# An attention and two-layer expert kernel: the low halves of the expert weights are formed on one engine instead of two

## The chip, the cores and the metric

The kernel runs on one core of one Trainium2 chip. The metric is the device time of one execution in microseconds. Three executions of the kernel before took 867.55, 1329.99 and 867.36 us, so the median is 867.55 us; the profiled execution took 865.88 us.

## The reference

Three stages follow each other on 3072 tokens (4 batches of 768) of 512 numbers.

```python
# 1. attention in chunks of 32 positions over 56 neighbours and 8 memory keys, 8 heads of 64
scores = scale * np.matmul(q_c, k_full.transpose(0, 1, 3, 2))
out[:, :, c_start:c_end] = np.matmul(softmax(scores), v_full)
# 2. a dense layer, 512 -> 2048 -> 512
h = x @ w_in
x = (h * np.cos(h)) @ w_out
# 3. eight experts, 512 -> 1024 -> 512, one per token, skipped where x @ w_skip <= 0
e_idx = np.argmax(xc @ w_gate, axis=1)
h = np.maximum(xc[mask] @ w1[e], 0.0)
y[mask] = gate_w[mask, None] * (h @ w2[e])
out[do_compute] = xc + y
```

## The kernel before

All products of the dense layer and of the experts are formed in three passes: each operand is split into a high part (rounded to fp32r) and a low part (what the rounding left), and high x high, high x low and low x high are added in PSUM. A weight piece is 128 x 1024 numbers (512 KB). For the experts, `plan_piece32` (L920) plans one piece `m`: SyncE loads it into a `raw` buffer (four of them, L930), ScalarE copies each half `s` of 512 columns to the high part (`copy`, L239), and a subtraction raw - high gives the low part (L939). Eight pieces make an expert; a piece with an even number holds a quarter of w1, one with an odd number a quarter of w2.

An expert's work on TensorE: L381 transposes its 128-token tiles of rows, L581 forms h for 128 hidden units of two tiles (12 matmuls of 256 columns; L1045 and L1055 do it for experts with one tile), ScalarE makes the high part `gh` (L1014), VectorE the low part `gl` (L1017), and L999 multiplies both by w2 (two groups of three matmuls of 512 columns, `gh` twice and `gl` last). L1087 on VectorE then joins the result with the tokens, and L1091 on GpSimd scatters it to `out`; each scatter waits for the one before it to have landed. L385 on VectorE makes the low part of the next expert's rows.

The order of every engine's queue is fixed ahead of time: each operation is a `Task` with an engine, an assumed duration and a key, and `Schedule.run` (L121) plays them through, always taking the ready task with the smallest key. The played order is written down, and the chip's engines then run their queues strictly in it. A changed engine or assumed duration of a task can therefore move other tasks too.

Before, the subtraction of half 1, and of both halves of the first `M_EARLY` = 18 pieces, is on VectorE; half 0 of the other 46 pieces is on GpSimd, in the same queue as the scatters L1091. Experts run in the order of their places 0 to 7; places 3 and 7 have one tile of tokens, place 0 treats its two tiles one after the other, the others take two tiles together. Place 2 is the first of which a half is subtracted on GpSimd.

Of the kernel before, what the change touches and what calls it, by code (L numbers as in the profile page):

```python
# [9 lines left out]
F32 = mybir.dt.float32  # L10
# [6 lines left out]
ALU = mybir.AluOpType  # L17
# [31 lines left out]
LEAD = 2.5  # L49
WARM = 12  # L50
EARLY = 16
M_EARLY = 18
RAW = 4
HOLD = (14, 16)
PACE = 8
# [42 lines left out]
class Schedule:  # L98
# [7 lines left out]
    def add(self, eng, dur, key, fn, after=(), new=(), use=(), table=None, nbytes=None):  # L106
        t = Task(eng, dur, key, fn, new, use, table, nbytes)
        for s in t.slots:
            s.users += 1
        for p in after:  # L110
            p.kids.append(t)
            t.wait += 1
        self.tasks.append(t)
        return t
# [75 lines left out]
def kernel(  # L190
# [13 lines left out]
    nc = tc.nc  # L204
# [33 lines left out]
    def copy(out, in_, scale=1.0):  # L238
        nc.scalar.activation(out=out, in_=in_, func=AF.Copy, scale=scale)  # L239
# [22 lines left out]
    def slot(name):  # L262
        return Slot(groups.setdefault(name, Group(1)))
# [5 lines left out]
    dve = lambda *a, **k: add("DVE", *a, **k)  # L269
    gps = lambda *a, **k: add("Pool", *a, **k)  # L270
# [20 lines left out]
    def warm_exp():  # L291
# [10 lines left out]
        out=first_slot, in0=eoff, scalar1=ident[:, 0:1], scalar2=None, op0=ALU.mult), [t_cb])  # L302
# [41 lines left out]
    for z in range(2):  # L344
        for i, name in enumerate(("k", "v")):
# [3 lines left out]
            use = [big[i]] if z else []  # L349
# [486 lines left out]
    w2_slot, w2_ready, w2_used, outs, regs = {}, {}, {}, [], {}  # L836
# [83 lines left out]
    def plan_piece32(m, key):  # L920

        o = {}
        s_raw, s_w = slot("raw"), slot("w")
        w2_slot[m] = s_w
        src = m % 2 * (NF2 // 2) + m % NF2 // 2

        def ld():
            o["r"] = pools["mp"][1].tile([P, 1024], F32, tag="raw", name="raw", bufs=RAW)
            piece = w12[bass.ds(regs[m // NF2] * NF2 + src, 1)]
            nc.sync.dma_start(out=o["r"], in_=piece.rearrange("o p c -> p (o c)"))  # L930

        def alloc():
            wt["x", m] = wp.tile([P, 2, 1024], F32R, tag="w", name="w", bufs=16)

        half = lambda s: o["r"][:, 512 * s:512 * s + 512]
        part = lambda s, i: wt["x", m][:, i, 512 * s:512 * s + 512]

        def lo(eng, s):
            eng.tensor_tensor(out=part(s, 1), in0=half(s), in1=part(s, 0).bitcast(F32), op=ALU.subtract)  # L939

        early = m < M_EARLY
        hold = [] if m < M_HOLD else [last["placed"]]
        w = mark(key, alloc, [last["mp"]] + hold, new=[s_w])
        after = [last["mp"], last["reg", m // NF2]] + ([w2_used[m - PACE]] if m >= PACE else [])
        x = load(key - 2, ld, P * 4096, after, new=[s_raw])
        w2_ready[m] = []
        for s in range(2):
            eng, put, dur = (nc.vector, dve, 0.6) if s or early else (nc.gpsimd, gps, 1.23)
            h = act(0.52, key + s * 0.5, lambda s=s: copy(part(s, 0), half(s)), [x, w], use=[s_raw, s_w])
            w2_ready[m].append(put(dur, key + s * 0.5, lambda s=s, eng=eng: lo(eng, s), [h], use=[s_raw, s_w]))  # L950

    def plan_rows(p, t, key, after):

# [179 lines left out]
    for c in range(NCH):  # L1133
        key = at[c // 2, NF - 1] + 1.7
# [35 lines left out]
    for p, t, j, key in todo:  # L1170
        mine = NF2 * p + 2 * (j if t is not None else j // 2) + 1
        while planned <= mine:
            plan_piece32(planned, keys[planned] - 5)
            planned += 1
        if t is None:
            plan_unit2(p, j, key)
        else:
            plan_pair(p, t, j, key)
# [156 lines left out]
```

## Time and profile before

| what | value |
|---|---|
| three executions | 867.55, 1329.99, 867.36 us |
| the profiled execution, whole | 865.88 us |
| its span, first to last instruction | 864.1 us |
| TensorE busy | 823.9 us, 95% |
| VectorE, ScalarE, GpSimd busy | 595.9, 525.5, 312.5 us |
| mean granted TensorE clock | 0.980 |
| DMA in all | 106.09 MB, mean 123 GB/s |

The attention and the dense layer take the span up to about 665 us; the experts run from there to 852 us. PE is TensorE, DVE VectorE, ACT ScalarE, POOL GpSimd and SP SyncE; a releaser behind an arrow is what ended the engine's idle time. Start times are microseconds from the span's start. A TensorE row's duration is modelled and overlaps the next row, so the distance between the starts of rows is what counts there.

### The profile page before, as it was taken

Reading aid. Unit: us, or ns where it says so; the run is one execution under the profiler, and the core shown is the slowest. Engines: PE = TensorE matmul, PEld = TensorE weight load, DVE = VectorE, ACT = ScalarE, POOL = GpSimd, SP = SyncE. Lnnn points to the kernel's source line nnn. Section 1 sums busy time; section 2 is a strip of 40 time slices with the busy share of each in tenths; the row PEclk is TensorE's granted clock in tenths of the full one; section 3 lists DMA queues with packets and bytes.
Section 4 is the critical chain, followed back from the end, with each engine's and each line's share of the span. In section 5 each row is a group of like instructions: output and inputs, shape, how many; then the busy total and the mean of one; then the engine's idle time right before and its main releaser. Section 6 shows DMA issues by size and latency. Waiting matters only on the chain.

```text
span 864.1 us, 17777 instructions
## 1 busy us (share of the span) xinstructions
PE 823.9 (95%) x6408; PEld 718.1 (83%) x6408; DVE 595.9 (69%) x1552; ACT 525.5 (61%) x1204; POOL 312.5 (36%) x376
## 2 busy tenths in 40 slices
PE   7799899999999999999999999999999899999884
PEld 4688788878888888888888888888888799989773
DVE  7778885799749376583956749376596476896761
ACT  6778876555757566565655757566666465665341
POOL 5456454333323223232232232223233114675441
PEclk9799999999999999999999999999999999999998
DMA  9449545722223131321322214121312466685530
GB/s 344 160 141 281 152 138 198 217 76 76 67 66 96 32 99 35 85 70 33 104 60 62 70 49 111 35 62 28 122 57 90 176 237 233 214 303 208 175 121 29
DMA packets 37201, 106.09 MB, mean 123 GB/s; under 512 B 6747, under 2 KB 7003, under 8 KB 36976
## 3 DMA queue, kind: packets, MB, share of 16 engines
q1 hardware_dynamic: 34064, 98.74, 37.1%
q0 software_dynamic: 3040, 6.13, 2.0%
q8 instruction: 52, 0.85, 0.4%
q14 instruction: 45, 0.37, 0.1%
HBM read 88.10 MB, written 20.77 MB: 126 GB/s over the span
## 4 chain that ended last, share of the span: by engine, by line
PE 79%; DVE 7%; ACT 4%; DMA 4%; issue 3%; POOL 1%; SPq 1%; DVEq 0%; POOLq 0%; ACTq 0%
PE pb L581 35%; PE py L585 26%; PE py L999 7%; PE pb L449 4%; PE pb L1045 2%; DVE junk L688 2%; PE pb L381 1%; DMA flat<-in_kt_dram 1%; DVE w L939 1%; ACT w L239 1%; PE pb L473 1%; DVE u L620 1%; DMA xg<-xs 1%; DMA more<-in_qt_dram 1%; DVE ki L609 1%
## 5 line engine op out<-in xcount | busy, mean ns | idle before, releaser
L581 PE MATMUL pb<-xh,w 128*128 128x256 f32 x1856 | 268.8, 288 | 7.5 <-ACT xh L239 3.9
L628 POOL TENSOR_TENSOR gl<-u,gh 128x256 fp32r<-128x256 f32 x192 | 146.8, 765 | 351.1 <-ACT gh L239 266.6
L581 PEld LDWEIGHTS pb<-xh,w 128*128 128x128 f32 x1856 | 249.6, 192 | 28.7 <-DVE u L620 6.5
L585 PE MATMUL py<-w,gh 128*128 128x512 f32 x768 | 244.9, 400 | 0.6 <-ACT yt L239 0.3
L688 DVE SCALAR_TENSOR_TENSOR junk<-yt,wg 128x512 bf16<-128x512 f32 x198 | 149.3, 754 | 7.4 <-ACT yt L239 4.9
L585 PE MATMUL py<-w,gl 128*128 128x512 f32 x384 | 150.8, 393 | 0.7 <-POOL gl L628 0.7
L581 PE MATMUL pb<-xl,w 128*128 128x256 f32 x928 | 149.7, 284 | 0.0
L585 PEld LDWEIGHTS py<-w,gh 128*128 128x128 f32 x768 | 132.4, 190 | 20.6 <-ACT gh L239 1.7
L609 DVE SCALAR_TENSOR_TENSOR ki<-pb,ki 128x256 f32<-128x256 f32 x192 | 80.5, 419 | 84.6 <-ACT ki L239 84.2
L620 DVE SCALAR_TENSOR_TENSOR u<-ki,pb 128x256 f32<-128x256 f32 x192 | 79.9, 417 | 75.0 <-ACT ki L616 72.7
L581 PEld LDWEIGHTS pb<-xl,w 128*128 128x128 f32 x928 | 128.6, 193 | 0.0
L239 ACT ACTIVATE ki<-pb 128x256 int32<-128x256 f32 x192 | 72.8, 380 | 88.1 <-PE pb L581 68.8
L613 ACT ACTIVATE ki<-ki 128x256 f32<-128x256 f32 x192 | 79.7, 416 | 62.2 <-DVE ki L609 62.0
L239 ACT ACTIVATE gh<-u 128x256 fp32r<-128x256 f32 x192 | 79.4, 414 | 58.4 <-DVE u L620 51.8
L939 DVE TENSOR_TENSOR w<-raw,w 128x512 fp32r<-128x512 f32 x82 | 85.8, 1060 | 21.0 <-ACT w L239 20.5
L585 PEld LDWEIGHTS py<-w,gl 128*128 128x128 f32 x384 | 72.3, 188 | 20.0 <-POOL gl L628 3.4
L239 ACT ACTIVATE w<-raw 128x512 fp32r<-128x512 f32 x128 | 74.9, 625 | 14.4 <-DMA raw<-in_w_dram 13.6
L616 ACT ACTIVATE ki<-ki 128x256 f32<-128x256 f32 x192 | 79.6, 415 | 4.6
L939 POOL TENSOR_TENSOR w<-raw,w 128x512 fp32r<-128x512 f32 x46 | 60.5, 1326 | 45.9 <-ACT w L239 45.4
L999 PE MATMUL py<-w,gh 128*128 128x512 f32 x224 | 72.8, 406 | 0.0
L560 POOL TENSOR_TENSOR w<-cv,w 128x512 fp32r<-128x512 f32 x32 | 41.2, 1290 | 38.3 <-ACT w L239 36.8
L999 PE MATMUL py<-w,gl 128*128 128x512 f32 x112 | 45.5, 406 | 5.3 <-DVE gl L1017 5.1
(152 smaller groups left out, 859.4 us busy)
## 6 DMA issues: line engine op xcount, KB each, us to landing
raw<-in_w_dram SPq DMA_DIRECT2D x64, 512.0 KB
k<-in_kt_dram SPq DMA_DIRECT2D x40, 256.0 KB
v<-in_vw_dram SPq DMA_DIRECT2D x40, 256.0 KB
st<-in_w_in_dram SPq DMA_DIRECT2D x16, 512.0 KB
st<-in_w_out_dram SPq DMA_DIRECT2D x16, 512.0 KB
out_dram<-yt SPq DMA_DIRECT2D x96, 64.0 KB
q<-in_qt_dram SPq DMA_DIRECT2D x21, 256.0 KB
xs<-fl SPq DMA_DIRECT2D x8, 528.0 KB
```

What stands on the lines that cost most here:

```text
L239: nc.scalar.activation(out=out, in_=in_, func=AF.Copy, scale=scale)
L560: nc.gpsimd.tensor_tensor(out=wt[f][:, i, 1, :], in0=o["f"], in1=wt[f][:, i, 0, :].bitcast(F32), op=ALU.subtract)
L581: nc.tensor.matmul(ph, w[:, i, ct, :], x[j][:, ct, :], start=(n == 0), stop=(n == len(todo) - 1))
L585: nc.tensor.matmul(py, g[i][:, t * P:t * P + P], w[:, j, :], start=(first and n == 0), stop=(last and n == 2))
L609: nc.vector.scalar_tensor_tensor(out=o["v"], in0=o["p"], scalar=INV2PI / W_SCALE, in1=o["k"], op0=ALU.mult, op1=ALU.subtract)
L613: nc.scalar.activation(out=o["v"], in_=o["v"], func=AF.Sin, scale=math.pi)
L616: nc.scalar.activation(out=o["v"], in_=o["v"], func=AF.Square, scale=math.sqrt(2.0))
L620: nc.vector.scalar_tensor_tensor(out=o["u"], in0=o["v"], scalar=1.0, in1=o["p"], op0=ALU.subtract, op1=ALU.mult)
L628: nc.gpsimd.tensor_tensor(out=o["g"][1], in0=o["u"], in1=o["g"][0].bitcast(F32), op=ALU.subtract)
L688: nc.vector.scalar_tensor_tensor(out=junk, in0=o["y"][:, 0:DM], scalar=1.0, in1=state["wg"][:, j, :], op0=ALU.mult, op1=ALU.mult, accum_ou ...
L939: eng.tensor_tensor(out=part(s, 1), in0=half(s), in1=part(s, 0).bitcast(F32), op=ALU.subtract)
L999: nc.tensor.matmul(ey[p, t], g[i][:, cols], w[:, j, 512 * (f % 2):512 * (f % 2) + 512], start=(f == 0 and q == 0), stop=(f == n - 1 and q ...
```

## The change

`M_EARLY` goes, and the subtraction L939 has one engine: all 128 of them (64 pieces, two halves) are on VectorE, none on GpSimd. The assumed duration that the planner uses for them becomes 0.62 us (it was 0.6 on VectorE, 1.23 on GpSimd).

```diff
-M_EARLY = 18
@@
-        def lo(eng, s):
-            eng.tensor_tensor(out=part(s, 1), in0=half(s), in1=part(s, 0).bitcast(F32), op=ALU.subtract)
-
-        early = m < M_EARLY
+        def lo(s):
+            nc.vector.tensor_tensor(out=part(s, 1), in0=half(s), in1=part(s, 0).bitcast(F32), op=ALU.subtract)
+
@@
         for s in range(2):
-            eng, put, dur = (nc.vector, dve, 0.6) if s or early else (nc.gpsimd, gps, 1.23)
             h = act(0.52, key + s * 0.5, lambda s=s: copy(part(s, 0), half(s)), [x, w], use=[s_raw, s_w])
-            w2_ready[m].append(put(dur, key + s * 0.5, lambda s=s, eng=eng: lo(eng, s), [h], use=[s_raw, s_w]))
+            w2_ready[m].append(dve(0.62, key + s * 0.5, lambda s=s: lo(s), [h], use=[s_raw, s_w]))
```

In the changed kernel's rows line numbers are 1 less (up to this function) or 3 less (behind it): the subtraction is L938, `gl` L1014, L385 is L384, L581 is L580, L999 is L996, and the scatter is L1088.

VectorE's queue while the expert of place 5 runs, before (`w<-raw,w` is the subtraction, `gl` the low part of an activation, `xl` that of the rows of place 6):

```order
L939 TENSOR_TENSOR w<-raw,w 128x512
L1017 SCALAR_TENSOR_TENSOR gl<-pb,gh 128x256
L939 TENSOR_TENSOR w<-raw,w 128x512
L1017 SCALAR_TENSOR_TENSOR gl<-pb,gh 128x256
L385 TENSOR_TENSOR xl<-pb,xh 128x4x128
L939 TENSOR_TENSOR w<-raw,w 128x512
L385 TENSOR_TENSOR xl<-pb,xh 128x4x128
L939 TENSOR_TENSOR w<-raw,w 128x512
L1017 SCALAR_TENSOR_TENSOR gl<-pb,gh 128x256 x2
```

The same place now:

```order
L938 TENSOR_TENSOR w<-raw,w 128x512 x2
L1014 SCALAR_TENSOR_TENSOR gl<-pb,gh 128x256
L938 TENSOR_TENSOR w<-raw,w 128x512 x2
L1014 SCALAR_TENSOR_TENSOR gl<-pb,gh 128x256
L938 TENSOR_TENSOR w<-raw,w 128x512
L384 TENSOR_TENSOR xl<-pb,xh 128x4x128
L938 TENSOR_TENSOR w<-raw,w 128x512
L384 TENSOR_TENSOR xl<-pb,xh 128x4x128
L938 TENSOR_TENSOR w<-raw,w 128x512 x2
L1014 SCALAR_TENSOR_TENSOR gl<-pb,gh 128x256 x2
```

Ahead of each `gl` there now stand two subtractions, both halves of a piece, where one stood.

GpSimd's queue over the experts of places 4 to 7, before (subtractions, and the scatters of finished rows):

```order
L1091 DMA out_dram<-ot,ri 3072x512
L939 TENSOR_TENSOR w<-raw,w 128x512 x8
L1091 DMA out_dram<-ot,ri 3072x512
L939 TENSOR_TENSOR w<-raw,w 128x512
L1091 DMA out_dram<-ot,ri 3072x512
L939 TENSOR_TENSOR w<-raw,w 128x512 x7
L1091 DMA out_dram<-ot,ri 3072x512
L939 TENSOR_TENSOR w<-raw,w 128x512
L1091 DMA out_dram<-ot,ri 3072x512
L939 TENSOR_TENSOR w<-raw,w 128x512 x7
L1091 DMA out_dram<-ot,ri 3072x512 x3
```

GpSimd's queue now, from the last rows of the dense layer to the end of the experts:

```order
L675 MEMSET yt 128x7
L676 COPY yt<-cb 128x1
L675 MEMSET yt 128x7
L676 COPY yt<-cb 128x1
L743 DMA xs<-yt,si 24704x528 x2
L1088 DMA out_dram<-ot,ri 3072x512 x14
```

GpSimd has only the fourteen scatters left; nothing stands behind one that waits.

TensorE's queue changes at one place, where the one-tile expert of place 3 hands over to place 4. Before (`cb,xg` is the transpose of place 4's second tile of rows):

```order
L381 MATMUL pb<-cb,xg 128x128 x4
L999 MATMUL py<-w,gh 128x512 x2
L999 MATMUL py<-w,gl 128x512
L1055 MATMUL pb<-cb,u 128x128 x2
L999 MATMUL py<-w,gh 128x512 x2
L999 MATMUL py<-w,gl 128x512
L581 MATMUL pb<-xh,w 128x256 x8
L581 MATMUL pb<-xl,w 128x256 x4
```

Now:

```order
L1052 MATMUL pb<-cb,u 128x128 x2
L996 MATMUL py<-w,gh 128x512 x2
L996 MATMUL py<-w,gl 128x512
L996 MATMUL py<-w,gh 128x512 x2
L996 MATMUL py<-w,gl 128x512
L380 MATMUL pb<-cb,xg 128x128 x4
L996 MATMUL py<-w,gh 128x512 x2
L996 MATMUL py<-w,gl 128x512
L996 MATMUL py<-w,gh 128x512 x2
L996 MATMUL py<-w,gl 128x512
L580 MATMUL pb<-xh,w 128x256 x8
L580 MATMUL pb<-xl,w 128x256 x4
```

The transpose and place 4's first h moved behind more of place 3's products; the count of matmuls is the same. On SyncE one load of rows (`xg`) there stands one weight load later, and ScalarE's copies keep their number.

## Rows read from the trace of the kernel before

**Rows 1.** The page: busy us, share of the span and instructions by engine

```profile
PE 823.9 (95%) x6408; PEld 718.1 (83%) x6408; DVE 595.9 (69%) x1552; ACT 525.5 (61%) x1204; POOL 312.5 (36%) x376
```

**Rows 2.** Stretches: length, busy us of PE, PEld, DVE, ACT, POOL; clock, DMA share, GB/s

```profile
700.00:720.00 20.00, 20.00 (x128) 18.04 (x127) 12.88 (x28) 10.95 (x27) 5.46 (x5) 1.00 0.63 213
...
780.00:800.00 20.00, 20.00 (x132) 18.08 (x131) 13.01 (x24) 11.87 (x29) 10.68 (x9) 1.00 0.58 201
800.00:820.00 20.00, 17.42 (x102) 15.60 (x102) 14.14 (x24) 7.59 (x18) 8.26 (x7) 0.91 0.50 164
820.00:840.00 20.00, 17.43 (x104) 15.36 (x102) 12.82 (x12) 8.12 (x18) 8.62 (x7) 0.91 0.43 148
```

**Rows 3.** Stretches, as rows 2: without and with GpSimd's subtractions, and behind the first wait

```profile
690.00:711.00 21.00, 21.00 (x140) 19.08 (x139) 17.14 (x48) 13.69 (x37) 2.15 (x2) 1.00 0.69 235
711.00:842.00 131.00, 125.64 (x794) 112.40 (x793) 97.01 (x147) 72.33 (x164) 70.55 (x55) 0.97 0.62 212
802.40:805.70 3.30, 2.97 (x10) 2.58 (x11) 3.00 (x6) 0.00 (x0) 0.00 (x0) 0.50 0.64 176
```

**Rows 4.** Groups, 690 to 711 us: busy us, mean ns | idle before, its enders

```profile
L939 DVE TENSOR_TENSOR w<-raw,w 128x512 fp32r<-128x512 f32 x16 | 10.4, 682 | 0.2
```

**Rows 5.** Groups, 711 to 842 us, columns as rows 4

```profile
L939 DVE TENSOR_TENSOR w<-raw,w 128x512 fp32r<-128x512 f32 x46 | 61.5, 1339 | 19.8 <-ACT w L239 19.5
L939 POOL TENSOR_TENSOR w<-raw,w 128x512 fp32r<-128x512 f32 x46 | 60.5, 1326 | 45.9 <-ACT w L239 45.4
...
L1017 DVE SCALAR_TENSOR_TENSOR gl<-pb,gh 128x256 fp32r<-128x256 f32 x36 | 15.1, 419 | 12.2 <-ACT gh L1014 12.1
```

**Rows 6.** Timeline of TensorE, 784 to 860 us: start, duration, instruction [idle before <-its ender]

```profile
791.57 1.12 PE L581 MATMUL pb<-xh,w 128*128 128x256 f32 x8
792.52 0.64 PE L581 MATMUL pb<-xl,w 128*128 128x256 f32 x4
793.00 0.63 PE L999 MATMUL py<-w,gh 128*128 128x512 f32 x2
...
794.39 1.12 PE L581 MATMUL pb<-xh,w 128*128 128x256 f32 x8
...
799.52 0.64 PE L999 MATMUL py<-w,gh 128*128 128x512 f32 x2
802.73 0.80 PE L999 MATMUL py<-w,gl 128*128 128x512 f32 x1 [2.58 <-DVE gl L1017]
...
804.60 1.62 PE L581 MATMUL pb<-xh,w 128*128 128x256 f32 x8
806.06 0.63 PE L581 MATMUL pb<-xl,w 128*128 128x256 f32 x4
```

**Rows 7.** Timeline of VectorE, around the first wait

```profile
793.94 0.69 DVE L939 TENSOR_TENSOR w<-raw,w 128x512 fp32r<-128x512 f32 x1 [2.40 <-ACT w L239]
...
796.65 5.69 DVE L939 TENSOR_TENSOR w<-raw,w 128x512 fp32r<-128x512 f32 x1 [1.68 <-ACT w L239]
802.26 0.41 DVE L1017 SCALAR_TENSOR_TENSOR gl<-pb,gh 128x256 fp32r<-128x256 f32 x1
```

**Rows 8.** Timeline of GpSimd, around the first wait

```profile
795.76 0.99 POOL L1091 DMA_INDIRECT out_dram<-ot,ri  x1 [5.91 <-DMA raw<-in_w_dram]
796.78 5.01 POOL L939 TENSOR_TENSOR w<-raw,w 128x512 fp32r<-128x512 f32 x4
```

**Rows 9.** Timeline of ScalarE, ahead of the first wait

```profile
795.41 1.15 ACT L239 ACTIVATE w<-raw 128x512 fp32r<-128x512 f32 x2 [1.28 <-DMA raw<-in_w_dram]
```

**Rows 10.** Timeline of VectorE, the second wait

```profile
823.32 6.18 DVE L939 TENSOR_TENSOR w<-raw,w 128x512 fp32r<-128x512 f32 x1 [1.60 <-ACT w L239]
```

**Rows 11.** Timeline of TensorE, around the second wait

```profile
826.70 0.63 PE L999 MATMUL py<-w,gh 128*128 128x512 f32 x2
...
831.77 1.68 PE L581 MATMUL pb<-xh,w 128*128 128x256 f32 x8
833.29 0.65 PE L581 MATMUL pb<-xl,w 128*128 128x256 f32 x4
```

## The prediction

> **What bounds the kernel now.** The page comes first: TensorE is busy 95% of the span, the others 69% and less [rows 1]. A gain can therefore come only from where TensorE isn't at its pace, and the change touches only the experts. So the second view is the table of stretches from 700 us on. TensorE is busy 20.00 of 20 us from 700 to 720 and from 780 to 800, and 17.4 of 20 in each of the stretches that begin at 800 and 820, where the granted clock is 0.91 [rows 2]. The third view, TensorE's timeline, shows why. In the regular pattern a unit's second product starts at 793.00 and the next h at 794.39, which is 1.39 us, and an h takes 792.52 - 791.57 = 0.95 us from its first part to its second; a whole unit, h to h, is 794.39 - 791.57 = 2.82 us. At 802.73 a matmul that reads `gl` has waited 2.58 us for VectorE [rows 6], and right behind it the clock is at the lower of its two levels, 1.2 GHz instead of 2.4 (0.50 granted from 802.4 to 805.7) [rows 3].
>
> VectorE's timeline names the culprit. The `gl` in question (L1017) starts at 802.26, behind a subtraction L939 that began at 796.65 and took 5.69 us [rows 7]. GpSimd ran four subtractions of its own from 796.78 to 801.79 in that time [rows 8], and VectorE's ended 0.55 us behind the last of them. The four had gathered behind a scatter that held GpSimd idle for 5.91 us [rows 8]. At 823.32 there is a twin of 6.18 us [rows 10].
>
> That this is a rule and not two accidents is seen in the groups. Where only VectorE subtracts (690 to 711 us), L939 takes 682 ns in the mean, 16 of them 10.4 us [rows 4]. Where GpSimd subtracts as well (711 to 842 us), VectorE's 46 take 1339 ns in the mean, 61.5 us in all [rows 5].
>
> The Trainium skill (SBUF — State Buffer, section "Who interferes with whom") says that a VectorE instruction with two SBUF inputs, as L939 has, contends with a GpSimd instruction that reads SBUF. The trace agrees, with 1339 against 682 ns.
>
> **The change, part by part.** *Removed: 46 subtractions on GpSimd* (60.5 us of it [rows 5]). GpSimd is no bound and keeps the scatters; nothing queues behind a waiting scatter any more but the next scatter, which waits for it anyway. Direct cost or gain: nothing.
>
> *Added: 46 subtractions on VectorE.* All 92 of the stretch now run there. At the price of the stretch without GpSimd, 10.4/16 = 0.65 us each [rows 4], that is 92 x 0.65 = 59.8 us, against 61.5 us that the 46 take now [rows 5]. So VectorE's load stays where it is, about 97 - 1.7 = 95 us of 131 [rows 3, 5]: it does twice the subtractions in the time that it now loses by waiting for the other engine. The price was measured with the same work around it: the copies, the loads (235 GB/s) and TensorE at full pace, 21.00 of 21 us [rows 3]. Its lower bound is the same 0.65 us, since nothing in the trace is faster; the upper one is the 1.34 us of rows 5, if something other than GpSimd lengthens it. I take 0.65.
>
> *Gained: the two waits.* The first: from 799.52 to the next h at 804.60 pass 5.08 us instead of 1.39, so 3.69 us are lost, and that h takes 806.06 - 804.60 = 1.46 instead of 0.95 us, 0.51 us more, which is the low clock [rows 6]. In all 4.20 us, of which 2.58 are the wait and 1.62 the clock. The second: 831.77 - 826.70 = 5.07, less 1.39 is 3.68; 833.29 - 831.77 = 1.52, less 0.95 is 0.57; in all 4.25 us [rows 11, 6]. Together **8.45 us**.
>
> *What is late next.* At the same place, with the new order: both halves of the piece copied from 795.41 on are there by 796.56 [rows 9]. Their two subtractions, which now stand ahead of `gl`, end at about 796.56 + 0.68 = 797.24, and `gl` at 797.24 + 0.42 = 797.66 [rows 4, 5]. TensorE reaches its product at 799.52 [rows 6], so there are 1.9 us in hand where before 2.7 were missing. TensorE therefore stays at its pace, and all of 8.45 us comes back.
>
> *Moved: the order of the tasks.* At the hand-over from place 3 to place 4 TensorE does the same matmuls in another order; I take nothing for it, because products of place 3 lie ahead of place 4's first h that need none of what was moved. If that cover is missing, the nearest row for a wait on VectorE is 2.58 us [rows 6]. One load of rows is issued one weight load later; the nearest row for a late load is ScalarE's 1.28 us [rows 9], and I take nothing. The planner's 0.62 for 0.6 us shifts a few subtractions by a neighbour in the last part of the dense layer, with nothing added there: nothing.
>
> **Sum.** The profiled execution took 865.88 us, 1.78 of it outside its span of 864.1. 865.88 - 8.45 = 857.4 us. The two executions of before that agree, 867.36 and 867.55, lie 1.5 and 1.7 us above the profiled one, so the same sum made from them gives 858.9 and 859.1. I predict 858.5 us, between the two, with 856 to 861 for this case alone.
>
> **The rivals.**
>
> *Late loads take the place of the port (part of the gain).* ScalarE waits 1.28 us for a `raw` transfer just ahead of the first stall [rows 9], and VectorE waited 2.40 us for a copy at 793.94 [rows 7]. With both halves ahead of `gl` in a strict queue, a load that comes more than the 1.9 us in hand too late stops TensorE again. For it: after each expert the loads restart late. Against it: L939 ends sooner, so a `raw` buffer comes free sooner and its next load starts sooner. If half of each wait stays, 1.3 us and the clock behind it 1.6 us, twice, 5.8 of 8.45 us are kept lost: 858.5 + 5.8 = 864.3 us. Chance 0.15.
>
> *Only one GpSimd instruction is to blame.* VectorE could have been held by GpSimd for one instruction, 5.01/4 = 1.25 us [rows 8], and for the rest by something that stays. Then 2.58 - 1.25 = 1.33 us of each wait and the clock behind it stay, 2 x (1.33 + 1.62) = 5.9 us: 858.5 + 5.9 = 864.4 us. For it: nothing in a single row splits the 5.69 us. Against it: VectorE's instruction ended 0.55 us behind the fourth, as if it had only then begun. Chance 0.05.
>
> The Trainium skill (same page and section) says that whichever engine issues second is blocked until the first one's instruction has finished; that would be one instruction, not four. The trace differs so far as it shows VectorE ending behind the run of four, after 5.69 us.
>
> *It does nothing.* If the long L939 were a label for a wait on late data, both waits would stay: 867.5 us. Against it: its release by ScalarE is marked ahead of its start, at both places [rows 7, 10]. Chance 0.05.
>
> *VectorE becomes the bound (slower).* If the 1339 ns were the price of L939 in this stretch because of the transfers or copies, the move would double it. Two units of TensorE take 2 x 2.82 = 5.64 us and need four L939 and two `gl`. At 0.65 us that is 4 x 0.65 + 2 x 0.42 = 3.44 us; it passes 5.64 from 1.2 us for an L939 on. At 1.34 it is 6.20, 0.56 us too much, 16 times in the four two-tile experts of places 2, 4, 5 and 6: 9 us. The two one-tile experts have at most half of TensorE's time, 2.82 us (an estimate from halving it), for the same pieces: 4 x 1.34 + 0.42 = 5.78, 2.96 us too much, 8 times: 24 us. 858.5 + 33 = 891 us. Against it stand the 682 ns of rows 4 with the same transfers around. Chance 0.03.
>
> *More than the two waits.* The rest of TensorE's time from 700 on is at its pace [rows 2], so there is hardly more: two or three microseconds at most. Chance 0.02.
>
> **Chances and range.** The forecast has 0.70, the rivals 0.15, 0.05, 0.05, 0.03 and 0.02. The range 856 to 865 us takes in the forecast and the first two rivals and leaves out the last three, about 0.1. A measurement of this kernel can tell about 2%, 17 us, from no change. Faster by more than that would need twice what the two waits hold: 0.01. Slower by more is the case in which VectorE becomes the bound: 0.03. Within 2%: 0.96.
>
> **What would show it.** Right: no L939 above about 0.8 us, 128 of them on VectorE with a mean near 0.68 us; VectorE's busy time near 595 us; GpSimd's 60 us lower; TensorE busy 19.8 or more of 20 us in every stretch between 700 and 835, the clock at 1.00 there, and no row of L996 (L999 before) with an idle time above 0.3 us. The first rival would show idle time of VectorE's L938 ended by ScalarE of more than 2.5 us and behind it a `gl` for which TensorE waits; the second an L938 of 3 us or more without GpSimd; the slower one a mean of L938 above 1.2 us. The prediction would be wrong if TensorE waited elsewhere, most likely at the hand-over from place 3 to place 4.

## The result, and the profile after

The changed kernel takes 856.54 us, the median of nine executions (854.24 to 858.99), against 867.55 us before. The ratio is 0.9882, with a 95% interval of 0.9852 to 0.9911, so it is 7.7 to 12.8 us faster, 10.2 in the middle. The 1329.99 us of one execution before belong to a disturbed execution and are in none of the ratios. The profiled execution took 858.50 us with a span of 856.6 us.

The page of the kernel after answers [rows 1]:

```profile
PE 819.2 (96%) x6408; PEld 715.4 (84%) x6408; DVE 590.3 (69%) x1598; ACT 525.4 (61%) x1204; POOL 251.9 (29%) x330
```

VectorE has 46 instructions more and is busy 5.6 us less. GpSimd lost 60.6 us of work.

The stretches of the kernel after answer [rows 2], with the same columns:

```profile
700.00:720.00 20.00, 20.00 (x131) 18.17 (x131) 15.20 (x39) 11.42 (x27) 1.18 (x1) 1.00 0.70 234
720.00:740.00 20.00, 20.00 (x131) 18.19 (x130) 14.43 (x34) 11.59 (x27) 1.96 (x2) 1.00 0.63 217
740.00:760.00 20.00, 19.96 (x132) 17.75 (x131) 14.92 (x27) 12.19 (x27) 1.94 (x2) 1.00 0.71 234
...
780.00:800.00 20.00, 20.00 (x131) 18.20 (x131) 14.63 (x34) 11.68 (x28) 1.96 (x2) 1.00 0.64 219
800.00:820.00 20.00, 20.00 (x131) 18.20 (x130) 14.12 (x30) 9.93 (x23) 1.96 (x2) 1.00 0.60 210
820.00:840.00 20.00, 20.00 (x137) 18.28 (x137) 11.49 (x21) 9.32 (x21) 2.15 (x2) 1.00 0.25 86
```

TensorE has no hole above 0.1 us left in the stretches shown between 700 and 840 us, and the clock stays at its upper level (1.00) there. The groups of VectorE from 711 to 835 us answer [rows 5]:

```profile
L938 DVE TENSOR_TENSOR w<-raw,w 128x512 fp32r<-128x512 f32 x92 | 59.8, 687 | 9.1 <-ACT w L238 7.1
L1014 DVE SCALAR_TENSOR_TENSOR gl<-pb,gh 128x256 fp32r<-128x256 f32 x37 | 15.6, 422 | 20.4 <-ACT gh L1011 19.5 <-issue 0.9
...
L977 DVE TENSOR_SCALAR ep<-xg,nm 128x8 f32<-128x8 f32 x8 | 2.0, 251 | 0.0
```

All 92 subtractions take 59.8 us, where 46 took 61.5, and one takes 687 ns in the mean where it took 1339. The longest of all 128 takes 960 ns.

How long the experts take is read from TensorE's timeline, from the start of the transposes for place 0's second tile to the start of the last matmul. Before:

```profile
688.73 1.30 PE L381 MATMUL pb<-cb,xg 128*128 128x128 f32 x8 [1.20 <-DMA xg<-xs]
...
851.58 0.18 PE L1265 MATMUL pb<-osum,ones 128*128 128x8 bf16 x1
```

After:

```profile
690.62 1.28 PE L380 MATMUL pb<-cb,xg 128*128 128x128 f32 x8 [1.48 <-DMA xg<-xs]
...
844.40 0.18 PE L1262 MATMUL pb<-osum,ones 128*128 128x8 bf16 x1
```

The stretch is 162.85 us before and 153.78 after, 9.07 us less. The two profiled executions as a whole differ by only 865.88 - 858.50 = 7.4 us, because the one of after reached this point 1.9 us later, in a part that the change doesn't touch. Over the traces of all runs here this point lies between 685 and 692 us, so one execution can differ from the next by several microseconds ahead of the experts.

### The profile page after: what moved, and what is told of

The parts are those of the page before. It is cut to its first block, busy times and chain, and to the rows that moved or that the text cites. A ratio compares the mean times of both kernels' runs of the same rounds, so it can differ in the third digit from the quotient of the medians.

```text
span 856.6 us, 17702 instructions
## 1 busy us (share of the span) xinstructions
PE 819.2 (96%) x6408; PEld 715.4 (84%) x6408; DVE 590.3 (69%) x1598; ACT 525.4 (61%) x1204; POOL 251.9 (29%) x330
## 4 chain that ended last, share of the span: by engine, by line
PE 81%; DVE 6%; DMA 5%; ACT 3%; issue 3%; SPq 1%; POOL 1%; DVEq 0%; POOLq 0%; ACTq 0%
PE pb L580 35%; PE py L584 26%; PE py L996 8%; PE pb L448 4%; PE pb L1042 3%; DVE junk L687 2%; PE pb L380 2%; DMA st<-in_w_in_dram 1%; DMA q<-in_qt_dram 1%; PE pb L472 1%; DVE u L619 1%; DMA flat<-in_kt_dram 1%; DVE cv L555 1%; DMA xg<-xs 1%; PE py L448 1%
## 5 line engine op out<-in xcount | busy, mean ns | idle before, releaser
L580 PE MATMUL pb<-xh,w 128*128 128x256 f32 x1856 | 267.3, 287 | 8.4 <-DVE u L619 4.6
L580 PEld LDWEIGHTS pb<-xh,w 128*128 128x128 f32 x1856 | 247.8, 191 | 29.5 <-DVE u L619 8.1
L580 PE MATMUL pb<-xl,w 128*128 128x256 f32 x928 | 149.9, 284 | 0.0
L580 PEld LDWEIGHTS pb<-xl,w 128*128 128x128 f32 x928 | 128.7, 193 | 0.2 <-DVE xl L384 0.2
L938 DVE TENSOR_TENSOR w<-raw,w 128x512 fp32r<-128x512 f32 x128 | 83.8, 690 | 11.1 <-ACT w L238 9.0
L996 PE MATMUL py<-w,gh 128*128 128x512 f32 x224 | 71.9, 402 | 0.0
L1088 POOL DMA_INDIRECT out_dram<-ot,ri x14 | 14.7, 1053 | 153.5 <-DVE ot L1084 118.2
L996 PE MATMUL py<-w,gl 128*128 128x512 f32 x112 | 43.8, 391 | 0.0
```

The source lines that it names most:

```text
L580: nc.tensor.matmul(ph, w[:, i, ct, :], x[j][:, ct, :], start=(n == 0), stop=(n == len(todo) - 1))
L938: nc.vector.tensor_tensor(out=part(s, 1), in0=half(s), in1=part(s, 0).bitcast(F32), op=ALU.subtract)
L996: nc.tensor.matmul(ey[p, t], g[i][:, cols], w[:, j, 512 * (f % 2):512 * (f % 2) + 512], start=(f == 0 and q == 0), stop=(f == n - 1 and q ...
```

## The experiments

One theory and three rivals stood at the start. The theory is the prediction's: GpSimd's subtractions hold VectorE's up, and four of them in a row, gathered behind a scatter that waits for the one before it, make TensorE wait. The rivals: VectorE is held for one instruction only, late data are to blame, or the new order of the tasks is.

Whole executions carry the spread of the part ahead of the experts. The stretch measured above, from the transposes for place 0's second tile to the last matmul, doesn't. For the one traced execution of each run it is:

| run | us |
|---|---|
| before, two traces | 162.85, 164.72 |
| the changed kernel | 153.78 |
| GpSimd only writes | 153.69 |
| the order of the neighbours | 154.82 |
| scatters out of the way | 156.41 |
| only the last expert on GpSimd | 153.82 |
| GpSimd's cut into 256 columns, into 128 | 154.35, 177.27 |
| a gap between GpSimd's subtractions | 169.14 |
| VectorE's cut into 256 columns | 167.89 |
| twice the work on VectorE | 188.01 |
| one load buffer fewer | 154.68 |

### GpSimd only writes

```diff
+            if eng is nc.gpsimd:
+                eng.memset(part(s, 1).bitcast(F32), 0.0)
+                return
             eng.tensor_tensor(out=part(s, 1), in0=half(s), in1=part(s, 0).bitcast(F32), op=ALU.subtract)
```

> The kernel before with each of GpSimd's 46 subtractions replaced by a memset of the same 128x512 tile: it writes and reads nothing from SBUF, in the same place of the same queue (the low part of half 0 of pieces 18 to 63 is left out, so the output lacks that correction). Theory (GpSimd's reads and VectorE's second SBUF input meet at a port): L939 on VectorE takes 0.68 us throughout, TensorE doesn't wait, about 857 us, although GpSimd's queue bunches as before. Rival (any GpSimd instruction, or late data, holds VectorE): L939's mean stays above 1.0 us, a row of several us stays, 862 to 867 us.

Measured: 856.90 us (853.54 to 859.18), ratio 0.9894 (0.9860 to 0.9929). GpSimd's and VectorE's timelines at one place, and their groups from 711 to 830 us:

```profile
788.99 3.35 POOL L940 MEMSET w<- 128x512 f32 x7
...
790.63 0.69 DVE L942 TENSOR_TENSOR w<-raw,w 128x512 fp32r<-128x512 f32 x1 [2.69 <-ACT w L239]
791.94 0.69 DVE L942 TENSOR_TENSOR w<-raw,w 128x512 fp32r<-128x512 f32 x1 [0.28 <-POOL w L940]
```

```profile
L942 DVE TENSOR_TENSOR w<-raw,w 128x512 fp32r<-128x512 f32 x45 | 31.2, 693 | 21.2 <-ACT w L239 19.2 <-issue 1.4 <-POOL w L940 0.3
L940 POOL MEMSET w<- 128x512 f32 x40 | 19.3, 541 | 0.0
```

Seven memsets ran in a row, and the subtractions that ran beside them took 0.69 us as elsewhere. So neither the queue of GpSimd, nor the copies, nor late loads make L939 long; GpSimd's reading of SBUF does. The memset is also shorter, 541 ns against 1326, so this run alone doesn't separate reading from length. The shorter subtractions below, which read, lengthened L939 in both forms, to 960 and 1453 ns in the mean, and those of 128 columns are no longer than a memset (526 ns). TensorE and VectorE ran the queues of the kernel before in this run (from 700 to 838 us their rows stand in the same order), so the gain isn't the new order either.

Another VectorE instruction was held by the memsets: L983 (L980 in the kernel before), which subtracts the largest of eight scores from each of the eight.

```profile
755.96 2.40 POOL L940 MEMSET w<- 128x512 f32 x5
...
756.13 2.26 DVE L983 TENSOR_SCALAR ep<-xg,nm 128x8 f32<-128x8 f32 x1
```

It takes 251 ns in the mean in the changed kernel (L977). Here it ended 0.03 us behind the last of five memsets, and two more of its nine rows, of 1.31 and 0.96 us, ended within 0.04 us of the end of such a run. So this form is held up by GpSimd's writing too.

### The order of the neighbours

```diff
-M_EARLY = 18
+M_EARLY = 64
```

> The kernel before with M_EARLY = 64: every subtraction on VectorE as in the change, but with the planner's 0.6 us in place of 0.62, so that neighbours stand in another order at some places. Theory (the place of the work counts, the order of neighbours doesn't): as the changed kernel, 855 to 859 us, no wait of TensorE above 0.3 us behind 692 us. Rival (part of the gain is the new order): 860 us or more.

Measured: 857.51 us (856.28 to 859.02), ratio 0.9905 (0.9876 to 0.9934), as the changed kernel. TensorE waits nowhere behind 692 us. The planner's 0.62 us and the order that follows from it cost or bring nothing that can be measured here; taking the subtractions off GpSimd does.

### Scatters out of the way

```diff
+    for p in range(1, E - 2):
+        if out_of.count(p) == 2:
+            sc.link(w2_ready[NF2 * (p + 2) + 4][0], outs[first_out[p] + 1])
     sc.run()
```

(`out_of` lists each scatter's expert, `first_out` the place of an expert's first scatter in `outs`.)

> The kernel before, with the second scatter of each two-tile expert (places 1 to 5) put four subtractions later in GpSimd's queue, so that the scatter ahead of it has landed by then; all 46 subtractions stay on GpSimd. Theory (the waits come from the runs of four that gather behind the waiting scatter; a single GpSimd subtraction only lengthens an L939 to 1.3 us, which VectorE can bear): mean L939 behind 711 us stays 1.2 to 1.4 us, none above 3 us, no wait of TensorE above 0.5 us, 857 to 861 us. Rival (VectorE's load or the contention as such costs the time): 864 to 868 us.

Measured: 857.33 us (857.01 to 861.96), ratio 0.9894 (0.9861 to 0.9926). The traced execution is the slowest of its five. Its groups, 711 to 838 us, and its longest wait of TensorE in that stretch:

```profile
L940 POOL TENSOR_TENSOR w<-raw,w 128x512 fp32r<-128x512 f32 x46 | 61.5, 1339 | 52.4 <-ACT w L239 51.7 <-PE pb L581 0.2
L940 DVE TENSOR_TENSOR w<-raw,w 128x512 fp32r<-128x512 f32 x45 | 51.8, 1155 | 20.1 <-ACT w L239 19.5 <-issue 0.3
```

```profile
773.11 0.50 PE L1000 MATMUL py<-w,gl 128*128 128x512 f32 x1 [0.64 <-DVE gl L1018]
```

All 46 subtractions stay on GpSimd, no more than two of them in a row, the mean on VectorE is still 1155 ns, and the time is that of the changed kernel within the intervals. The runs behind the waiting scatter thus cost most of the time. What is left of the contention isn't quite free: the experts of the traced execution take 156.41 us, 2.6 more than in the changed kernel. Three of the numbers expected were missed: the mean is below 1.2 us, one row of 3.76 us stayed (two GpSimd subtractions in a row), and the wait is 0.64 instead of at most 0.5 us.

### Only the last expert on GpSimd

```diff
-M_EARLY = 18
+M_EARLY = 56
```

> The kernel before with M_EARLY = 56: only the 8 halves of the last expert's pieces stay on GpSimd, the other 120 subtractions are on VectorE. Theory (each run of GpSimd subtractions behind a late scatter costs one wait of 4.2 us): the wait near 800 us is gone, the one near 827 us stays; 4.2 us slower than the changed kernel, about 861 us, with one L939 of 5 to 6 us. Rival (the gain came from the total load or from the new order of tasks): no wait is left or both are, so about 857 or about 866 us.

Measured: 854.27 us (853.32 to 855.75), ratio 0.9860 (0.9825 to 0.9894): neither the theory's 861 nor a wait. Timelines of GpSimd, VectorE and TensorE:

```profile
814.51 5.54 POOL L939 TENSOR_TENSOR w<-raw,w 128x512 fp32r<-128x512 f32 x4
...
818.30 1.75 POOL L939 TENSOR_TENSOR w<-raw,w 128x512 fp32r<-128x512 f32 x1
```

(The second row is the last of the four.)

```profile
814.76 4.13 DVE L939 TENSOR_TENSOR w<-raw,w 128x512 fp32r<-128x512 f32 x1 [1.04 <-ACT w L239]
818.81 0.41 DVE L1017 SCALAR_TENSOR_TENSOR gl<-pb,gh 128x256 fp32r<-128x256 f32 x1
```

```profile
819.28 0.50 PE L999 MATMUL py<-w,gl 128*128 128x512 f32 x1
```

The run of four is there, but VectorE was done at 818.89, 0.59 us behind the start of the fourth, which took 1.75 us instead of 1.3. So VectorE came through there, and the fourth was held up in turn. `gl` was done at 819.22, when TensorE was just ready for it. So it isn't the run that costs 4.2 us but the hold, and this place bears about 4 us of it. The step of my expectation that failed is that a run of four holds for all four. The rival that the total load cost the time had also expected no wait here; the run before this one speaks against it, since all 46 stayed on GpSimd there. Against the changed kernel (0.9852 to 0.9911) the intervals overlap, so this isn't shown to be faster; none of the kernels here is.

### A second trace of before

No edit.

> The kernel before, unchanged, for a second trace of it. Theory (whether VectorE is held for three or for four GpSimd subtractions is decided anew in each execution, and only four make TensorE wait): the runs of four on GpSimd stand at the same places, L939 rows of 4 to 6.2 us, but the number of TensorE's waits is not always two: between none and three, each worth 4.2 us. Rival (it is fixed by the program): the same two waits of 2.6 us at the same two places.

Measured: 866.32 us in one execution. TensorE's timeline, the three longest waits behind 700 us:

```profile
739.45 0.50 PE L999 MATMUL py<-w,gl 128*128 128x512 f32 x1 [1.37 <-DVE gl L1017]
...
803.67 0.50 PE L999 MATMUL py<-w,gl 128*128 128x512 f32 x1 [2.59 <-DVE gl L1017]
...
830.55 0.50 PE L999 MATMUL py<-w,gl 128*128 128x512 f32 x1 [2.08 <-DVE gl L1017]
```

VectorE's timeline of the last of them, and GpSimd's:

```profile
824.22 5.94 DVE L939 TENSOR_TENSOR w<-raw,w 128x512 fp32r<-128x512 f32 x1 [1.35 <-ACT w L239]
```

```profile
824.58 5.03 POOL L939 TENSOR_TENSOR w<-raw,w 128x512 fp32r<-128x512 f32 x4
```

At 739 us there is a wait that the first trace didn't have, since VectorE was held there for 5.33 us this time and for 4.07 in the first. So the number of waits differs between executions, as the theory had it. That each is worth 4.2 us was wrong: behind the wait of 1.37 us the granted clock stays at 1.00 (739 to 745 us). From the transposes at 687.63 to the last matmul at 852.35 this execution took 164.72 us, 10.94 more than the changed kernel. VectorE's instruction had started 0.36 us ahead of GpSimd's subtractions, during the scatter, and was still held to the end of all four.

### Shorter instructions on GpSimd

Cut into two of 256 columns:

```diff
-            eng.tensor_tensor(out=part(s, 1), in0=half(s), in1=part(s, 0).bitcast(F32), op=ALU.subtract)
+            n = 256 if eng is nc.gpsimd else 512
+            for k in range(0, 512, n):
+                eng.tensor_tensor(out=part(s, 1)[:, k:k + n], in0=half(s)[:, k:k + n],
+                                  in1=part(s, 0).bitcast(F32)[:, k:k + n], op=ALU.subtract)
```

> The kernel before with each of GpSimd's subtractions cut into two of 256 columns, same order. Theory (VectorE is held out until GpSimd's run of instructions that follow each other ends): runs of eight short instructions hold VectorE as long as runs of four did; longest L939 still 5 to 7 us, its mean on VectorE behind 711 us still about 1.3 us, time as before or a little slower, 866 to 870 us. Rival (VectorE is held for one GpSimd instruction only): no L939 above about 1.5 us, mean near 1.0 us, TensorE's two waits shrink to nothing, 857 to 860 us.

Measured: 856.35 us (853.90 to 861.70), ratio 0.9900 (0.9855 to 0.9945): the theory missed, and the rival's time came, just below its range. The traced execution is the fastest of its four. GpSimd's timeline, and the groups from 711 to 842 us:

```profile
793.40 8.44 POOL L941 TENSOR_TENSOR w<-raw,w 128x256 fp32r<-128x256 f32 x10
```

```profile
L941 POOL TENSOR_TENSOR w<-raw,w 128x256 fp32r<-128x256 f32 x90 | 76.2, 873 | 14.7 <-ACT w L239 14.5
...
L941 DVE TENSOR_TENSOR w<-raw,w 128x512 fp32r<-128x512 f32 x45 | 43.2, 960 | 21.5 <-ACT w L239 20.7 <-issue 0.3
```

Beside this run of ten no row of VectorE's subtraction is longer than 1.56 us (the longest of all is 2.27 us). The engines took turns. It looked as if short instructions on GpSimd cured it. Three further runs tested that.

Cut into four of 128 columns (the same edit with `n = 128`):

> The kernel before with each of GpSimd's subtractions cut into four of 128 columns. Theory (short instructions on GpSimd let VectorE in between): no L939 above 2.1 us, mean on VectorE behind 711 us at most the 0.96 us of the cut into two, no wait of TensorE above 0.3 us, 854 to 859 us. Rival (it was a chance of that order; or a fixed cost per instruction makes GpSimd the late one): rows of 3 us and more, or TensorE waiting for GpSimd's halves, 860 us or more.

Measured: 878.60 us (877.32 to 879.59), ratio 1.0181 (1.0119 to 1.0242); the theory missed. Groups from 711 to 855 us, and timelines of GpSimd, VectorE and TensorE:

```profile
L941 POOL TENSOR_TENSOR w<-raw,w 128x128 fp32r<-128x128 f32 x181 | 89.1, 526 | 25.2 <-ACT w L239 24.9
L941 DVE TENSOR_TENSOR w<-raw,w 128x512 fp32r<-128x512 f32 x45 | 65.3, 1453 | 18.1 <-ACT w L239 12.9 <-POOL w L941 2.6 <-issue 2.2
```

```profile
806.40 8.43 POOL L941 TENSOR_TENSOR w<-raw,w 128x128 fp32r<-128x128 f32 x20
```

```profile
807.14 8.24 DVE L941 TENSOR_TENSOR w<-raw,w 128x512 fp32r<-128x512 f32 x1
```

```profile
816.97 0.80 PE L1002 MATMUL py<-w,gl 128*128 128x512 f32 x1 [4.97 <-DVE gl L1020]
```

One VectorE instruction was held through eighteen GpSimd instructions of 0.46 us (the median). A short instruction on GpSimd is no cure.

A gap between them, by a memset of a spare 128x64 tile, which reads nothing:

```diff
             eng.tensor_tensor(out=part(s, 1), in0=half(s), in1=part(s, 0).bitcast(F32), op=ALU.subtract)
+            if eng is nc.gpsimd:
+                eng.memset(spare, 0.0)
```

> The kernel before with a memset of a spare 128x64 tile behind each of GpSimd's subtractions, so that no two of them follow each other directly; each keeps its 512 columns. Theory (VectorE loses the port at the joint of two GpSimd subtractions that follow each other directly, and gets it where something lies between): no L939 above 2.0 us (one GpSimd subtraction and its own 0.68), mean on VectorE behind 711 us 1.1 to 1.35 us, no wait of TensorE above 0.3 us, about 857 us. Rival (the length of GpSimd's instruction is what matters, as the cut into 256 columns might also mean): rows of 4 us and more stay, with one or two waits of TensorE, 861 to 867 us.

Measured: 866.78 us (862.39 to 872.46), ratio 0.9998 (0.9967 to 1.0029); the theory of the joint missed. VectorE's and GpSimd's timelines:

```profile
825.83 6.31 DVE L940 TENSOR_TENSOR w<-raw,w 128x512 fp32r<-128x512 f32 x1 [1.54 <-ACT w L240]
```

```profile
826.29 1.30 POOL L940 TENSOR_TENSOR w<-raw,w 128x512 fp32r<-128x512 f32 x1
827.52 0.15 POOL L942 MEMSET spare<- 128x64 f32 x1
827.64 1.30 POOL L940 TENSOR_TENSOR w<-raw,w 128x512 fp32r<-128x512 f32 x1
```

From 827.59 to 827.64 no GpSimd instruction that reads ran, and VectorE still didn't come through.

VectorE's own instruction cut into two of 256 columns (the first diff of this part with `n = 512 if eng is nc.gpsimd or early else 256`):

> The kernel before with VectorE's subtractions of pieces 18 to 63 cut into two of 256 columns; GpSimd's keep 512. Theory (what counts is the length of the instruction on GpSimd): VectorE is still held over three or four of GpSimd's, rows of 4 us and more stay, two or three waits of TensorE of 2 us and more, 863 to 869 us. Rival (two short instructions of either engine are enough for the engines to take turns): no VectorE row above 2.7 us, 856 to 860 us.

Measured: 871.03 us (868.23 to 876.61), ratio 1.0114 (1.0040 to 1.0189). VectorE's and TensorE's timelines:

```profile
803.02 5.78 DVE L941 TENSOR_TENSOR w<-raw,w 128x256 fp32r<-128x256 f32 x2 [0.49 <-issue]
```

```profile
739.88 0.80 PE L1002 MATMUL py<-w,gl 128*128 128x512 f32 x1 [4.46 <-DVE gl L1020]
```

Cutting VectorE's side doesn't help; that holds of several microseconds stay is as the theory had it, though the time is above its 863 to 869 us. Shown by these four: the hold can last over runs of GpSimd's reading instructions and not only over one. Open: why VectorE comes through between them in the cut into 256 columns and, now and then, behind the third of 512, and not in the cut into 128 or with the gap. No run here tells whether lengths, phases or something else decide it.

### Twice the work on VectorE

```diff
-            nc.vector.tensor_tensor(out=part(s, 1), in0=half(s), in1=part(s, 0).bitcast(F32), op=ALU.subtract)
+            for _ in range(1 if m < 18 else 2):
+                nc.vector.tensor_tensor(out=part(s, 1), in0=half(s), in1=part(s, 0).bitcast(F32), op=ALU.subtract)
```

> The changed kernel with every subtraction of pieces 18 to 63 done twice on VectorE, the second time with the same result (92 more of them, none on GpSimd). Theory (VectorE has 5.64 - 3.44 = 2.2 us in hand for each two units of a two-tile expert, and four more at 0.60 to 0.65 us need 2.4 to 2.6; in the one-tile experts it has none): VectorE becomes the bound behind 711 us, mean of the subtraction stays 0.68 us, TensorE waits for VectorE in many small pieces, 865 to 880 us. Rival (VectorE has room to spare and was no bound anywhere): within 2 us of the changed kernel, 855 to 859 us.

Measured: 890.44 us (890.14 to 891.48), ratio 1.0289 (1.0250 to 1.0327). Groups of VectorE from 711 to 860 us, and two stretches:

```profile
L939 DVE TENSOR_TENSOR w<-raw,w 128x512 fp32r<-128x512 f32 x173 | 115.6, 687 | 4.5 <-ACT w L238 1.2
```

```profile
740.00:760.00 20.00, 17.63 (x105) 15.16 (x104) 19.08 (x32) 8.39 (x18) 0.86 (x1) 0.91 0.53 176
760.00:780.00 20.00, 15.38 (x77) 12.77 (x76) 19.08 (x39) 8.88 (x23) 1.70 (x3) 0.83 0.62 192
```

VectorE is now busy 19.08 of 20 us and TensorE waits for it, at a clock of 0.83 to 0.91. Two subtractions of 0.65 us are as good as one of 1.30, so this run stands for the prediction's rival in which VectorE becomes the bound: it had worked out 891 us for 1.34 us a piece. That the times agree is in part luck: the rival's sum has no term for the low clock that the stretches show, and with 1.30 us for 1.34 it gives 887 us. My expectation of 865 to 880 us for this run was too low; its sum has no term for the clock either. How much of the difference that is wasn't separated.

### One load buffer fewer

```diff
-RAW = 4
+RAW = 3
```

> The changed kernel with three raw buffers instead of four, so that every load starts one piece later. Theory (in the changed kernel TensorE has about 1.9 us in hand at the places behind an expert's end, and the loads are the next to be late): TensorE waits at some of these places, 860 to 870 us, with VectorE's subtractions waiting for ScalarE and ScalarE for transfers, and the subtraction still at 0.68 us. Rival (loads have ample room): no wait of TensorE above 0.5 us, 855 to 859 us.

Measured: 859.12 us (854.13 to 860.97), ratio 0.9932 (0.9896 to 0.9967). The waits of the traced execution, 690 to 850 us (engine, line <- releaser: us in total, times, longest):

```profile
ACT w L238 <- DMA raw<-in_w_dram: 15.4, 19, 2.2
DVE w L938 <- ACT w L238: 12.8, 17, 2.1
```

ScalarE waits for loads up to 2.2 us and VectorE behind it, and TensorE waits nowhere in that execution. The loads have room; whether one buffer fewer costs a microsecond or two can't be told, since the intervals of this kernel and of the changed one overlap (the experts take 0.9 us more in its one trace).

## Why the prediction was right, point by point

**The forecast and the range.** 858.5 us was forecast and 856.54 measured, inside 856 to 865 and at the lower end of 856 to 861 that stood for the forecast's own case. It is within 2%, the case given 0.96. The direct sum was 857.4 us; the 1.1 us added to it, for the two executions that lay above the profiled one, led away from the measured median. All of this lies within the spread of the nine executions, 854.24 to 858.99 us.

**The added work.** The sum put 92 subtractions at 0.65 us, 59.8 us; they take 59.8 us. The row from the part where GpSimd doesn't subtract [rows 4] gave the price that holds in the changed kernel behind 711 us too. One sign was missed, that no row of it lies above about 0.8 us: the longest takes 0.96 us. VectorE's busy time was forecast near 595 us and is 590.3. Most of that difference is a term that the sum doesn't have: L980, a small instruction, takes 2.0 us behind 711 us (L977) where it took 6.2.

**The two waits.** Both are gone and the clock stays up. The sum had 8.45 us; the experts became 9.07 us shorter against the first trace, and 10.94 against the second. The mechanism was right, and its size was taken from one execution that had two waits; the other one has three. Against these traces the term was too small, by 0.6 to 2.5 us. That this is why the measured 10.2 us is more than 8.45 isn't shown, since 8.45 lies within the interval of 7.7 to 12.8 us. The case "more than the two waits" was given 0.02, and the second trace shows it in part: the prediction looked at one trace in which nothing else was late and not at whether the next execution would repeat it.

One link of the chain isn't in the row that the prediction named. It is that the scatter ahead of the first wait was held by the scatter before it. Rows 8 name a load as its releaser, and in the second trace the row of the same place names `gl`. At the second wait of the first trace the row does name the landing of a scatter (5.44 us). The run with the scatters put later, in which the runs of four are gone, bears the reading out.

**What is late next.** The forecast had 1.9 us in hand for `gl` behind the end of place 4. VectorE's timeline of after, at that place:

```profile
797.78 0.42 DVE L1014 SCALAR_TENSOR_TENSOR gl<-pb,gh 128x256 fp32r<-128x256 f32 x1 [0.20 <-ACT gh L1011]
...
801.91 0.42 DVE L1014 SCALAR_TENSOR_TENSOR gl<-pb,gh 128x256 fp32r<-128x256 f32 x1
```

And TensorE's, where the two are used:

```profile
800.80 0.64 PE L996 MATMUL py<-w,gh 128*128 128x512 f32 x2
...
803.62 0.63 PE L996 MATMUL py<-w,gh 128*128 128x512 f32 x2
```

The first is done at 798.20, 2.6 us ahead of 800.80 (1.9 were forecast), and what it waited for last was `gh`, not a subtraction. The second, of the next unit, is done at 802.33, 1.3 us ahead of 803.62. The step was right: it is enough.

**The rivals.** Late loads didn't take GpSimd's place; with one buffer fewer they still don't stop TensorE. That only one GpSimd instruction holds VectorE is refuted by the hold through all four in both traces of before, and through eighteen short ones. That it does nothing is refuted by the time. VectorE isn't the bound at 0.65 us a piece; it is at twice the work. That the time then is what was worked out is luck in part, as said there; where in between it becomes the bound wasn't tried.

**The edits taken at nothing.** The changed order at the hand-over from place 3 to place 4, the moved load and the planner's 0.62 us show no wait: TensorE is busy 19.96 of 20 us from 740 to 760, the other order of neighbours gave the same time within the intervals, and the memset run took as little with the order of the kernel before.

## What to carry to other kernels

Before dividing elementwise work between VectorE and GpSimd, compare the mean of the same instruction on VectorE with and without GpSimd at work: here 46 instructions on each of the two engines cost VectorE as much (61.5 us) as all 92 without GpSimd (59.8 us). Here it was less the mean that hurt than the longest hold ahead of something that TensorE needs, and that arose where GpSimd's queue let work pile up behind a wait; either take the work away or take the wait out of its way. Size such a loss from more than one trace, since which of the holds reaches TensorE can differ from execution to execution.

## What the runs showed of the hardware

- A VectorE subtraction with both inputs in SBUF can be held through many GpSimd instructions that read SBUF, not only the one that it meets: four of 1.25 us (rows of 5.69 to 6.31 us) and eighteen of 0.46 us (8.24 us). In two of these rows it had started 0.60 us (at 823.32 [rows 10], with GpSimd's four from 823.92 on) and 0.36 us ahead of the first of the four, during a scatter on GpSimd; a scatter alone doesn't lengthen it (in the changed kernel two took 1.28 us beside one, from 728.20 us on). The Trainium skill (SBUF — State Buffer, section "Summary: rules for kernel authors") has the second one blocked until the first finishes; these rows differ from that, since VectorE stayed blocked through the GpSimd instructions behind the first.
- The hold goes the other way too: where VectorE came through at the start of a GpSimd subtraction, that one took 1.75 us instead of 1.30 us.
- GpSimd instructions that only write, seven memsets in a row, didn't lengthen it: 693 ns in the mean. The same page (section "Who interferes with whom") says so of a VectorE instruction with two SBUF inputs, and this run agrees.
- A tiny VectorE instruction suffers as well, and from memsets too: 2.26 us beside five of them, in the row shown above. In the kernel before, from 711 to 842 us, L980 took 779 ns in the mean on 128x8 numbers; it takes 251 ns after (L977, shown above):

```profile
L980 DVE TENSOR_SCALAR ep<-xg,nm 128x8 f32<-128x8 f32 x8 | 6.2, 779 | 0.0
```

- Cutting GpSimd's instruction into halves let the engines take turns in the one trace taken (the mean on VectorE 960 ns, time as the changed kernel), and cutting it into quarters made it worse than before (878.60 us). Why is open.
- Behind the first wait of TensorE of 2.6 us in the first trace the granted clock was 0.50 for 3.3 us [rows 3], the lower level; that made a loss of 2.6 into one of 4.2 us. Behind the wait of 1.37 us in the second trace it stayed at 1.00.
